# The keys' scales through PSUM in a fused DeltaNet and gated feed-forward kernel

## The chip, the cores and the metric

The kernel runs on one core of one Trainium2 chip. The metric is the device time of one execution in microseconds (us). Three runs of the kernel before took 640.12, 641.81 and 644.32 us; their median is 641.81.

The core's engines work beside each other, each through its own queue in order: PE (matmuls and transposes, results to PSUM), DVE (vector), ACT (activations and copies), POOL (GpSimd), and SP, which here only issues DMAs. They wait for each other through semaphores.

## What is computed

The first part is a DeltaNet layer over 4 batches, 8 heads, 768 steps and heads of 48 numbers; its output, 3072 tokens by 384, goes through a feed-forward layer with the gate h·cos(h) and 2048 hidden features.

```
k_n = k / (np.linalg.norm(k, axis=-1, keepdims=True) + 1e-06)
state = np.zeros((B, H, D, D))
for t in range(S):
    kt, vt, bt = (k_n[:, :, t], v[:, :, t], beta[:, :, t, None])
    y[:, :, t] = np.einsum('bhd,bhde->bhe', q[:, :, t], state)
    v_old = np.einsum('bhde,bhd->bhe', state, kt)
    state = state + bt[:, :, :, None] * np.einsum('bhd,bhe->bhde', kt, vt - v_old)
x = y.transpose(0, 2, 1, 3).reshape(B * S, H * D)
h = x @ w_in
out = (h * np.cos(h)) @ w_out
```

## The kernel before

**Stages.** The 768 steps are cut into 24 units `n` of 32 steps; two units make a pair `m`, and a pair of units is also one block `p` of 256 tokens of the feed-forward layer, so there are 12 blocks. For a unit the kernel loads k, q and v, turns k and q (`turn`, `turn_out`, or from unit 8 on `turn_blocks` on DVE), forms products of keys with keys and queries (`gram`, L652), inverts a triangular 32 by 32 system per head, and solves, updates the state and reads it (`through_state` L907, `right_side` L924, `solve` L979, `solve_out` L991, `update` L1004, `update_out` L1012, `within`). The inversion of the first pair is made by repeated doubling on PE and DVE (L691 to L756), that of the second for half its size, its first columns on DVE, and from then on it runs column by column on POOL: `invert` makes a product (L856, tile `part`) and subtracts it (L863, tile `z`). Its input passes through DRAM (`gram_put`, `gram_get`, tile `gb`), as does its result (`put`, `get`, tile `zt`).

The feed-forward layer of block 0 and of the input side of block 1 is plain (`hidden`, L1076, and `output`, L1274). From then on both of its matrix products are made with fewer multiplications: sums of inputs (`x_sum` L1165), factors on PE (`layer`, L1250), sums of results (`layer_add` L1267), sums of gated blocks (`left_sum` L1348) and of weights (`right_sum` L1361), products on PE (`product`, L1332) and their collection (`collect`, L1371 on ACT, L1384 on DVE). The gate is made by L1113 and L1129 on ACT and L1120 and L1132 on DVE. The weights arrive as 28 tiles (`weights`) and are converted by ACT (L525, L529), DVE (L533) and POOL (`narrow_add`, L537).

**Order.** `Order.LINE` lists all tasks in one order that was written down beforehand; `Order.run` emits them in it, and each engine gets its instructions in that order. `Order.OTHER` says which tasks run on the second of two engines. Nothing is scheduled when the program is built, except the waits: an instruction waits for what it depends on, and for two engines on one PSUM bank the dependency is taken by the bank, not by the columns.

**PSUM.** `p_out` is one bank of 512 columns, declared as [128, 2, 256]. Until the feed-forward output begins, PE runs filler matmuls into it (`keep_warm`, L492), into columns 0 to 255. `output` uses columns 0 to 383, `product` columns 0 to 191 or 256 to 447 by turns. Columns 448 to 511 are not used. A product of the output side has two parts of four matmuls; the next product waits until the previous one is collected.

**Scales of the keys.** For a pair (for the first two pairs: for each unit, "part"), ACT squares the keys (L554), DVE sums them (L559, tile `ksum`), POOL takes the root (L571, tile `knrm`, 8 heads for one or two units: 8 or 16 columns). `scale` on DVE then adds 1e-6 (L582), squares (L584), takes the reciprocal (L585), multiplies by beta (L587, tile `bs`) and spreads that over odd and even quarters (L590, tile `bz`); all five read and write SBUF. There are 14 such groups. `bs` and `bz` go into `gram_keys` (L664, L673) and `solve_out` (L991). `weigh` multiplies v by the norms in place (L607, 128 by 768), from unit 8 on after three small copies (L603, L605) that set the norms of odd heads in place.

Of the kernel before, what the change touches and what calls it, by code (L numbers as in the profile page):

```python
# [10 lines left out]
FP = mybir.dt.float32  # L11
I32 = mybir.dt.int32
U32 = mybir.dt.uint32
ALU = mybir.AluOpType
# [225 lines left out]
def kernel(  # L240
# [32 lines left out]
    nc = tc.nc  # L273

    B, H, S, D = q.shape
# [17 lines left out]
    const = ctx.enter_context(tc.tile_pool(name="const", bufs=1))  # L293
# [3 lines left out]
    work = ctx.enter_context(tc.tile_pool(name="work", bufs=2))  # L297
# [27 lines left out]
    def half(i):  # L325
        return slice(DP * i, DP * i + DP)
# [105 lines left out]
    odd = consts[:, 128 + C : 130 + C]  # L432
# [9 lines left out]
    for b in range(B):  # L442
        nc.gpsimd.dma_start(
            out=bq[C * b : C * b + H].rearrange("p n t -> p (n t)"), in_=beta[b]
# [2 lines left out]

    halves = const.tile([128, 2, H], FP, name="halves")
    nc.vector.memset(halves, 0.5)
    tiny = const.tile([128, 2, H], FP, name="tiny")  # L450
    nc.vector.memset(tiny, 1e-6)
    halfpi = const.tile([128, 1], FP, name="halfpi")
    nc.vector.memset(halfpi, math.pi / 2.0)

# [9 lines left out]
    bt = const.tile([128, NU, H], FP, name="bt")  # L464
# [18 lines left out]

    HM = DM // 2
    p_out = psum.tile([128, 2, 256], FP, name="p_out", tag="o", bufs=1)


    out_begun = []
# [89 lines left out]
    def scale(m, part):  # L578

        n = part.stop - part.start  # L580
        bs, bz, knrm = (t[:, part] for t in scales[m])
        nc.vector.tensor_tensor(out=knrm, in0=knrm, in1=tiny[:, 0:n], op=ALU.add)  # L582
        krec = work.tile([128, 2, H], FP, name="krec")[:, 0:n]
        nc.vector.tensor_tensor(out=krec, in0=knrm, in1=knrm, op=ALU.mult)  # L584
        nc.vector.reciprocal(krec, krec)  # L585
        first = 2 * m + part.start
        nc.vector.tensor_tensor(  # L587
            out=bs, in0=bt[:, first : first + n], in1=krec, op=ALU.mult
        )
        nc.vector.tensor_tensor(  # L590
            out=bz,
            in0=bs[:, :, :, None].to_broadcast([128, n, H, 2]),
            in1=odd[:, None, None, :].to_broadcast([128, n, H, 2]),
            op=ALU.mult,
        )

    def weigh(m):

        vp, knrm = vps[m], scales[m][2]
        if 2 * m >= PLAIN_TURNS:  # L600

            t = work.tile([128, 2, H], FP, name="krec")
            nc.vector.tensor_copy(t[:, :, 0::2], knrm[:, :, 0::2])  # L603
            for i in range(2):
                nc.vector.tensor_copy(t[half(i), :, 1::2], knrm[half(1 - i), :, 1::2])  # L605
            knrm = t
        nc.vector.tensor_tensor(  # L607
            out=vp,
            in0=vp,
            in1=knrm[:, :, :, None].to_broadcast([128, 2, H, D]),  # L610
            op=ALU.mult,
        )

    def turn(n, tag):
# [346 lines left out]
    first, spare = {}, {}  # L961
# [431 lines left out]
    def store(p, i, cols=slice(0, DM)):  # L1393
# [7 lines left out]
        for b in range(B):  # L1401
# [9 lines left out]
            x=2, x_sum=XS, turns=2, g=GATES, o=2, o_out=2,  # L1411
# [59 lines left out]
    def unit(n):  # L1471
# [20 lines left out]
        if n < 4 or not second:  # L1492
            add(("square", m, a), "ACT", 0.2 + 0.37 * width, lambda: norms_square(m, part),
                [("k", 2 * m + x) for x in range(part.start, part.stop)],
                makes=[("g", ("ksq", m, a))])
            add(("sum", m, a), "DVE", 0.2 + 0.4 * width, lambda: norms_sum(m, part),
                [("square", m, a)], makes=[("ksum", ("ksum", m, a))], uses=[("ksq", m, a)])
            add(("norms", m, a), "POOL", 0.4 + 1.28 * width, lambda: norms_root(m, part),
                [("sum", m, a)] + ([("norms", m, 0)] if a else []),
                makes=[] if a else [("scales", ("scales", m))], uses=[("ksum", m, a)])  # L1500
            add(("scale", m, a), "DVE", 1.1, lambda: scale(m, part),
                [("norms", m, a), ("beta",) if n < PLAIN_TURNS else ("beta_home",)])
        scaled = ("scale", m, a if n < 4 else 0)
        if second:
            add(("weigh", m), "DVE", 1.1 if n < PLAIN_TURNS else 1.5, lambda: weigh(m),
                [("v", n - 1), ("v", n), ("scale", m, 0), scaled])
# [419 lines left out]
```

## Time and profile before

| | |
|---|---|
| profiled execution | 641.69 us |
| its span on the core | 639.9 us, so 1.8 us around it |
| granted clock of PE, mean | 0.996 |
| median of three runs | 641.81 us |
| POOL L856 / L863, inversion, 317 each | 142.0 / 141.0 us busy |
| PE L1332 (two groups) / L1250 (four) / L1076 (one of several) | products and factors of the feed-forward layer, the costliest on PE |
| DVE waiting for PE before L1384 | 29.9 us in 34 waits |
| POOL L571, 14 roots | 36.1 us busy, 2.58 us each |
| DMA | 50.36 MB, mean 79 GB/s |

By stages (busy us of each stretch):

| stretch, us | PE | DVE | ACT | POOL |
|---|---|---|---|---|
| 28 to 64 | 32.40 of 36 | 31.96 | 22.59 | 18.97 |
| 64 to 112 | 44.01 of 48 | 29.21 | 25.35 | 38.35 |
| 112 to 172 | 60.00 of 60 | 51.76 | 29.62 | 45.95 |
| 172 to 215 | 40.21 of 43 | 37.67 | 14.78 | 37.73 |
| 215 to 300 | 85.00 of 85 | 68.76 | 40.60 | 72.34 |
| 300 to 400 | 100.00 of 100 | 87.07 | 46.27 | 83.30 |
| 400 to 640 | 236.02 of 240 | 173.19 | 106.79 | 128.16 |

A line of a profile view names the kernel's line (L582 is line 582), the engine, the operation and its tiles as out<-in. In the timeline the first two columns are start and length in us from the start of the span, xN the number of instructions merged into the line (a matmul in fp32 is recorded as two), and what stands in brackets is the idle time of the engine before it and what ended that.

### The profile page before, as it was taken

What the parts mean: (1) busy time and instruction counts of PE and PEld (TensorE: products, weight loads), DVE (VectorE), ACT (ScalarE), POOL (GpSimd) and SP (SyncE); (2) the same over time, 40 slices, a digit from 0 to 9 for tenths busy, and PEclk for the clock granted to TensorE, in tenths of its full rate; (3) what the DMA queues carried; (4) which work ended last, traced back from release to release, by engine and by line L of the source; (5) the groups of instructions that cost most, each with busy time, mean ns of one, the idle gap of its engine ahead of it and who ended that gap; (6) DMA issues with size and microseconds to landing.
All of it is one profiled execution on the core that took longest, in us unless ns stands there. A gap on an engine that the chain in (4) does not pass through costs nothing.

```text
span 639.9 us, 24164 instructions
## 1 busy us (share of the span) xinstructions
PE 618.1 (97%) x10172; PEld 576.0 (90%) x10172; DVE 499.1 (78%) x1026; ACT 298.0 (47%) x528; POOL 435.4 (68%) x779
## 2 busy tenths in 40 slices
PE   6898998999999899999999999999999999999997
PEld 5677878897799899999999999999999999999997
DVE  5799646979788887887988888888888786656682
ACT  3566555555234553634642634743643553545440
POOL 5335977688788888789688888886883883112231
PEclk9999999999999899999999999999999999999999
DMA  7978555843632534424454445243304202000001
GB/s 155 253 157 229 106 128 110 181 87 58 117 46 51 114 50 74 85 55 78 93 79 86 66 73 92 53 64 67 73 3 78 45 2 42 19 3 26 1 24 26
DMA packets 209380, 50.36 MB, mean 79 GB/s; under 512 B 200920, under 2 KB 204280, under 8 KB 209272
## 3 DMA queue, kind: packets, MB, share of 16 engines
q1 hardware_dynamic: 157564, 33.91, 28.2%
q10 hardware_dynamic: 51404, 14.36, 10.8%
q8 instruction: 80, 1.31, 0.8%
q0 software_dynamic: 304, 0.54, 0.4%
q14 instruction: 28, 0.23, 0.1%
HBM read 38.55 MB, written 10.22 MB: 76 GB/s over the span
## 4 chain that ended last, share of the span: by engine, by line
PE 76%; POOL 8%; DMA 5%; DVE 4%; SPq 4%; issue 2%; ACT 0%; POOLq 0%; DVEq 0%
PE p_out L1332 28%; PE p_h L1250 26%; PE p_h L1076 5%; POOL part L856 4%; POOL z L863 4%; PE p_kq L907 3%; PE p_s L1004 3%; PE p_kq L1034 2%; PE p_u L979 2%; PE p_g L652 2%; SPq L396 2%; PE p_h L1332 2%; DMA gb<-g_dr 1%; DMA kp<-in_k_dram 1%; PE p_z L1055 1%
## 5 line engine op out<-in xcount | busy, mean ns | idle before, releaser
L856 POOL TENSOR_TENSOR part<-z,gb 128x126 f32<-128x126 f32 (+24 forms) x317 | 142.0, 448 | 47.0 <-DMA gb<-g_dr 11.7
L863 POOL TENSOR_TENSOR z<-z,part 128x126 f32<-128x126 f32 (+24 forms) x317 | 141.0, 445 | 24.9
L1332 PE MATMUL p_out<-w_out,g_ffn 128*128 128x192 f32 x672 | 123.7, 331 | 0.0
L1332 PEld LDWEIGHTS p_out<-w_out,g_ffn 128*128 128x128 f32 x672 | 108.8, 192 | 1.2 <-DVE g_ffn L1132 0.2
L1129 ACT ACTIVATE turns<-turns,halfpi 128x512 f32<-128x512 f32 x96 | 68.2, 719 | 56.8 <-DVE turns L1120 44.0
L1332 PE MATMUL p_out<-w_sum,g_ffn 128*128 128x192 f32 x496 | 89.8, 329 | 0.2 <-DVE o L1384 0.2
L1250 PE MATMUL p_h<-x_sum,w_in 128*128 128x128 f32 x640 | 83.9, 277 | 1.9 <-POOL x_sum L1165 1.9
L1113 ACT ACTIVATE turns<-g_ffn,quarter_turn 128x512 int32<-128x512 f32 x70 | 50.1, 720 | 69.6 <-DVE g_ffn L1267 23.3
L1250 PEld LDWEIGHTS p_h<-x_sum,w_in 128*128 128x128 f32 x640 | 79.0, 192 | 2.8 <-POOL x_sum L1165 2.1
L1332 PEld LDWEIGHTS p_out<-w_sum,g_ffn 128*128 128x128 f32 x496 | 79.5, 190 | 1.1 <-issue 0.4
L1267 DVE TENSOR_TENSOR g_ffn<-g_ffn,p_h 128x512 f32<-128x512 f32 x80 | 54.1, 680 | 18.5 <-PE p_h L1250 17.4
L1120 DVE SCALAR_TENSOR_TENSOR turns<-g_ffn,turns 128x512 f32<-128x512 f32 x70 | 55.6, 801 | 12.1 <-ACT turns L1113 12.0
L1132 DVE TENSOR_TENSOR g_ffn<-turns,g_ffn 128x512 f32<-128x512 f32 x70 | 53.2, 770 | 4.3 <-ACT turns L1129 4.2
L1047 ACT COPY y<-p_kq 32x384 f32<-32x384 f32 x96 | 45.1, 470 | 20.9 <-PE p_kq L1034 16.9
L1250 PE MATMUL p_h<-x_sum,in_sum 128*128 128x128 f32 x400 | 52.9, 277 | 0.0
L1250 PEld LDWEIGHTS p_h<-x_sum,in_sum 128*128 128x128 f32 x400 | 49.4, 192 | 0.9
L1384 DVE SCALAR_TENSOR_TENSOR o<-p_out,o 128x192 f32<-128x192 f32 x74 | 25.2, 352 | 30.3 <-PE p_out L1332 29.9
L1076 PE MATMUL p_h<-x_ffn,w_in 128*128 128x128 f32 x384 | 46.6, 278 | 1.1 <-DVE part L856 1.1
L1076 PEld LDWEIGHTS p_h<-x_ffn,w_in 128*128 128x128 f32 x384 | 44.2, 192 | 2.3 <-issue 1.2
L571 POOL TENSOR_TENSOR knrm<-ksum,halves 128x16 f32<-128x16 f32 (+1 forms) x14 | 36.1, 2580 | 14.8 <-DVE ksum L559 14.8
L1348 POOL TENSOR_TENSOR g_ffn<-g_ffn,g_ffn 128x512 f32<-128x512 f32 x19 | 27.2, 1434 | 23.2 <-PE p_out L1332 19.4
L1250 PE MATMUL p_h<-x_ffn,w_in 128*128 128x128 f32 x320 | 42.4, 278 | 0.0
(164 smaller groups left out, 1073.4 us busy)
## 6 DMA issues: line engine op xcount, KB each, us to landing
g_ffn<-in_moe_w_out_dram SPq DMA_DIRECT2D x13, 384.0 KB
g_ffn<-in_moe_w_in_dram SPq DMA_DIRECT2D x7, 512.0 KB
vp<-in_v_dram SPq DMA_DIRECT2D x68, 48.0 KB
gb<-g_dr SPq DMA_DIRECT2D x12, 256.0 KB
kp<-in_k_dram SPq DMA_DIRECT2D x120, 24.0 KB
g_ffn<-in_moe_w_in_dram ACTq DMA_DIRECT2D x5, 512.0 KB
zt<-z_dr SPq DMA_DIRECT2D x68, 32.0 KB
out_dram<-o ACTq DMA_DIRECT2D x11, 192.0 KB
```

Of the source, the lines that this page charges most:

```text
L571: nc.gpsimd.tensor_tensor(out=scales[m][2][:, part], in0=sums[m, part.start][:, 0:n], in1=halves[:, 0:n], op=ALU.pow,)
L856: eng.tensor_tensor(out=part, in0=z[:, 0:rows, j, None].to_broadcast(shape), in1=a[:, j, None, j + 1 :].to_broadcast(shape), op=ALU.mult,)
L863: eng.tensor_tensor(out=behind, in0=behind, in1=part, op=ALU.subtract)
L1047: nc.scalar.copy(by_parity(y[quarter(b)]), p_kq[quarter(b ^ 1), :, b % 2])
L1076: nc.tensor.matmul(p_h[:, i], w_in[:, t, (4 * k + i) * 128 : (4 * k + i + 1) * 128], xts[p][:, t, unit * 128 : (unit + 1) * 128], start=(i ...
L1113: nc.scalar.activation(turns[p, f], hidden_of(p, f), AF.Identity, bias=quarter_turn, scale=TURN)
L1120: nc.vector.scalar_tensor_tensor(out=r, in0=hidden_of(p, f), scalar=TURN, in1=t, op0=ALU.mult, op1=ALU.subtract,)
L1129: nc.scalar.activation(r, r, AF.Sin, bias=halfpi, scale=2.0 * math.pi)
L1132: nc.vector.tensor_tensor(out=place(p, f), in0=step_of(rests.pop((p, f)), f), in1=step_of(hidden_of(p, f), f), op=ALU.mult,)
L1250: nc.tensor.matmul(p_h[:, e], in_block(*w)[:, e], x_of(p, b), start=new and e == 0, stop=True, skip_group_check=True,)
L1267: nc.vector.tensor_tensor(out=part_of(p, to), in0=part_of(p, one), in1=part_of(p, two), op=op)
L1332: nc.tensor.matmul(p_o, left(p, part, a)[:, e % 4], right(e, b), start=(e == 0), stop=(e == FT // 2 - 1), skip_group_check=True,)
```

## The change

`krec` moves from a tile of its own in SBUF into the unused columns of `p_out`: 64 columns, of which a group takes 8 or 16 at a place that goes round. `knrm` is no longer changed in place; 1e-6 is added inside the squaring, which now takes two operations (the second adds again and multiplies), and inside `weigh`. `bz` is made from `krec` and beta directly, by two operations with `odd` as a scalar for each partition, one for each of the two columns. `scale` has six operations on DVE for five, each with at most one input from SBUF; `weigh` has the same number, its last a scalar_tensor_tensor of two SBUF inputs. The constant tile `tiny` and its memset go. The order of tasks is the same.

```diff
-    tiny = const.tile([128, 2, H], FP, name="tiny")
-    nc.vector.memset(tiny, 1e-6)
...
     p_out = psum.tile([128, 2, 256], FP, name="p_out", tag="o", bufs=1)
+    spare_out = p_out[:, 1, HM:]
...
         bs, bz, knrm = (t[:, part] for t in scales[m])
-        nc.vector.tensor_tensor(out=knrm, in0=knrm, in1=tiny[:, 0:n], op=ALU.add)
-        krec = work.tile([128, 2, H], FP, name="krec")[:, 0:n]
-        nc.vector.tensor_tensor(out=krec, in0=knrm, in1=knrm, op=ALU.mult)
+
+        at = (2 * m + part.start) % 4 * 2 * H
+        krec = spare_out[:, at : at + n * H].rearrange("p (u h) -> p u h", h=H)
+        nc.vector.tensor_scalar(krec, knrm, 1e-6, None, op0=ALU.add)
+        nc.vector.scalar_tensor_tensor(
+            out=krec, in0=knrm, scalar=1e-6, in1=krec, op0=ALU.add, op1=ALU.mult
+        )
         nc.vector.reciprocal(krec, krec)
         first = 2 * m + part.start
-        nc.vector.tensor_tensor(
-            out=bs, in0=bt[:, first : first + n], in1=krec, op=ALU.mult
-        )
-        nc.vector.tensor_tensor(
-            out=bz,
-            in0=bs[:, :, :, None].to_broadcast([128, n, H, 2]),
-            in1=odd[:, None, None, :].to_broadcast([128, n, H, 2]),
-            op=ALU.mult,
-        )
+        beta_here = bt[:, first : first + n]
+        nc.vector.tensor_tensor(out=bs, in0=beta_here, in1=krec, op=ALU.mult)
+        for x in range(2):
+            nc.vector.scalar_tensor_tensor(
+                out=bz[:, :, :, x], in0=krec, scalar=odd[:, x : x + 1], in1=beta_here,
+                op0=ALU.mult, op1=ALU.mult,
+            )
...
-        nc.vector.tensor_tensor(
+        nc.vector.scalar_tensor_tensor(
             out=vp,
-            in0=vp,
-            in1=knrm[:, :, :, None].to_broadcast([128, 2, H, D]),
-            op=ALU.mult,
+            in0=knrm[:, :, :, None].to_broadcast([128, 2, H, D]),
+            scalar=1e-6,
+            in1=vp,
+            op0=ALU.add,
+            op1=ALU.mult,
         )
```

## The prediction, made before the result

> **What bounds the kernel now.** I read the page first: its busy times and its chain.
>
> ```profile
> PE 618.1 (97%) x10172; PEld 576.0 (90%) x10172; DVE 499.1 (78%) x1026; ACT 298.0 (47%) x528; POOL 435.4 (68%) x779
> PE 76%; POOL 8%; DMA 5%; DVE 4%; SPq 4%; issue 2%; ACT 0%; POOLq 0%; DVEq 0%
> ```
>
> PE is busy nearly throughout and is three quarters of the chain, so a microsecond counts only if it makes PE start its next matmul earlier or later. From 112 us until its last matmul the PE timeline shows three idle gaps (0.78 at 172, 1.94 at 214, 0.20 at 440), 2.9 us together: there, whatever stalls PE is added one for one.
>
> Next I asked for the lines of the small operations (duration ns, min/median/max).
>
> ```profile
> L584 DVE TENSOR_TENSOR krec<-knrm x14: 166/175/1222, 11.4 to 450.0; 128x16 f32<-128x16 f32 x10, 128x8 f32<-128x8 f32 x4
> L585 DVE RECIPROCAL krec<-krec x14: 202/252/253, 11.6 to 450.2; 128x16 f32<-128x16 f32 x10, 128x8 f32<-128x8 f32 x4
> L673 DVE TENSOR_TENSOR g<-p_g,bs x22: 380/416/426, 34.0 to 485.7; 128x256 f32<-128x256 f32 x22
> ```
>
> With two inputs from SBUF (L584) an operation is sometimes seven times its median; with one (L585), or one of two from PSUM (L673), never. The timeline shows what it is then waiting for.
>
> ```profile
> 52.47 5.04 POOL L537 TENSOR_TENSOR w_in<-w_in,g_ffn 128x512 uint32<-128x512 uint32 x4 [0.70 <-DVE w_in L533]
> 53.12 0.67 DVE L582 TENSOR_TENSOR knrm<-knrm,tiny 128x16 f32<-128x16 f32 x1
> 53.82 1.22 DVE L584 TENSOR_TENSOR krec<-knrm 128x16 f32<-128x16 f32 x1
> 55.36 0.93 DVE L587 TENSOR_TENSOR bs<-bt,krec 128x16 f32<-128x16 f32 x1
> 56.32 1.23 DVE L590 TENSOR_TENSOR bz<-bs,consts 128x32 f32<-128x32 f32 x1
> 57.48 0.16 DVE L856 TENSOR_TENSOR part<-z,gb 128x15 f32<-128x15 f32 x1
> ```
>
> Four POOL additions run back to back, and one DVE operation gets through behind each. The scale group takes 4.4 us here; an undisturbed one (124.59) takes 1.1.
>
> **The change, part by part.** *Length of a group.* Five operations become six: the undisturbed starts are 0.20, 0.21, 0.29 and 0.21 us apart and the last takes 0.19; the new sixth adds one more 0.2, so 1.3 us for 16 columns a partition, 1.24 for 8. Nothing in this trace writes PSUM from DVE; L1384, which reads 192 columns of PSUM in 0.36 us, lies on the slope of SBUF operations (0.17 for 16 columns, 0.28 for 128), so I take no surcharge. Bounds: 0 and, if every write cost as much again as the operation, +0.8. Thirteen groups pay 0.2 us more; DVE's own idle time (22% of the span) covers that, and without that cover it would be 2.6 us. The scaling of v (L607) becomes a scalar_tensor_tensor of the same shape: L1120, such a form on SBUF, takes 0.68 for 512 columns, as does the tensor_tensor L1132; nothing. The removed memset is 0.07 us before PE has work.
>
> *Relief at 53.12.* In DVE 3.1 us. Of this PE can recover the two gaps it has there, 1.08 us before 59.72 and 1.21 before 63.84: at most 2.3. But what follows in DVE's queue is L856 and L863, the inversion's products, with both inputs in SBUF. The new group would end at 54.45; the additions end at about 53.73, 54.99, 56.25 and 57.51, so the first three products get through at 55.0, 56.3 and 57.55, and the fourth, which started at 58.10 before, at 57.55. Gain: 0.55 us, between 0 and 2.3. I take 0.55, since these products are the form that was held.
>
> *New waits.* The intermediate now lies in the bank of p_out, and in the built program the group's first operation waits for the last p_out matmul ahead of it, and the next p_out matmul waits for the group's last operation. I set each of the fourteen groups beside the p_out matmuls. Where DVE arrives first:
>
> ```profile
> 364.35 0.38 DVE L582 TENSOR_TENSOR knrm<-knrm,tiny 128x16 f32<-128x16 f32 x1
> 365.67 0.73 DVE L924 SCALAR_TENSOR_TENSOR rhs<-p_kq,consts,vp 128x192 f32<-128x192 f32 x2
> 365.43 1.47 PE L1332 MATMUL p_out<-w_out,g_ffn 128*128 128x192 f32 x8
> 368.61 0.68 PE L979 MATMUL p_u<-rhs,zt 64*64 64x48 f32 x32
> 372.10 0.89 PE L1004 MATMUL p_s<-u,kp 64*64 64x96 f32 x32
> ```
>
> At 364.35 the group must wait until the product ends at 366.90; it ends at 368.3. Queued behind it are L924's four, 1.4 us: the right side is ready at 369.7, and PE's solve, at 368.61, is 1.1 us late. Then u (L991) ends near 374.0 where 372.1 wanted it: up to 2.1 in all. I take 1.6. At 330.74 the wait is until 332.53; the group ends at 333.9, and behind it L1165, L1267 and the collect L1384 end at 335.05, while PE's next product, which waits for that collect, began at 334.14: 1.0 (0 to 1.85, the whole lag). At 287.97 the wait is 1.75 us, but PE's next product began at 292.22 and the collect would be done at 291.5: nothing. At 88.01 the wait is 0.6: the state update L1012 moves from 89.47 to 90.0, and PE's L652 already waits for it: 0.5 (0 to 0.6).
>
> Where PE arrives first:
>
> ```profile
> 34.93 1.13 PE L492 MATMUL p_out<-o 128*128 128x256 f32 x4
> 35.80 0.15 DVE L582 TENSOR_TENSOR knrm<-knrm,tiny 128x8 f32<-128x8 f32 x1
> 124.59 0.16 DVE L582 TENSOR_TENSOR knrm<-knrm,tiny 128x16 f32<-128x16 f32 x1
> 124.82 2.75 PE L1274 MATMUL p_out<-w_out,g_ffn 128*128 128x384 f32 x8
> ```
>
> The first row is two filler matmuls; the second, at 35.46, must wait for the group of 35.80, until 37.04 plus the 0.15 us by which PE followed DVE's L991 at 47.33. PE's queue is solid from 28.7 to 47 and DVE waits for PE at 39.61, so this is 1.7 us (0 to 1.7). At 124.82 the product must wait until 126.0: 1.1 (0 to 1.3); PE has no gap between 109 and 172. The other groups have room: at 53.12 PE's filler comes at 55.50, at 189.66 the product at 192.61, at 213.64 at 216.56, at 423.30 at 425.51, at 449.78 at 452.14. The first three lie ahead of 28.68, where PE stood idle 1.26 us for q from DRAM; that wait covers the 1.9 us by which the filler at 10.58 and the transposes behind it are held, except for what passes 1.26 (0 to 0.6; I take 0, since their product is wanted only at 15.90).
>
> Sum: 1.7 − 0.55 + 0.5 + 1.1 + 1.0 + 1.6 = +5.35 us. The profiled execution took 641.69, a span of 639.9 and 1.8 around it, 0.1 from the median of 641.81: I forecast **647.0**.
>
> One thing the sum leaves out is the clock: over 212.0 to 215.4 PE was busy 1.46 us of 3.40, and over 215.4 to 219.0 the granted clock was 0.53. The stalls above are up to 1.7 us in one place. Each such stretch costs about 1.7 us (half of 3.4). The Trainium skill (TensorE: Matmul & The Clock Gate, Why this matters for your kernels) asks for no idle gaps over about 3 us; by that none of the stalls here would cost clock, and the sum would stay. The trace goes against it: the drop came behind a gap of 1.94 us, though none came behind the 2.67 us before 14.83.
>
> **Rivals.** *Relief wins* (not slower): if the products let through at 55 to 57.5 are not held, PE gets 2.3 us at 64, and if DVE drifts by half a microsecond against PE, the wait at 88.01 falls away and those at 124.82 and 330.74 halve. Then 1.7 − 2.3 + 0 + 0.5 + 0.5 + 0 = +0.4 with the right side at 364 hidden too: 642. For it: PE's own gaps at 59.72 and 63.84. Against: L856 and L863 have the form of the held operations. It decides once the inversion's first product starts before 56.
>
> *Clock drops* (slower by over 1%): two of the new stalls pull the clock down for 3.4 us each, +3.4: 650.4. For: the row at 215.4. Against: the gap at 14.83, and that the longest new stall is 1.7. It decides from PE being busy under 45% of one 3.4 us stretch.
>
> *The change relieves nothing*: if an operation with one PSUM operand is held like the others, the group at 53.12 stays at 4.4 us and the waits remain: +5.9, 647.6. Against it stand the three rows on L584, L585 and L673.
>
> **Chances.** About 1% (6.4 us: below 635.4, above 648.2) is what a measurement of this kernel can tell from no change. The sum has 0.55: most of its bounds lie under 648.2, so 0.40 within and 0.15 above. Relief wins 0.20: 0.16 within, and 0.04 faster, which would need every held operation to have been on PE's path. Clock drops 0.17, all slower. No relief 0.08: 0.05 within, 0.03 slower. Together faster 0.04, within 0.61, slower 0.35. The range reaches from the relief case with a microsecond below it, 641, to the clock case with half a microsecond above, 651.
>
> **What would show it.** In the profile of after: the group at about 55 us takes 1.3 us and none of its operations over 0.3; the first inversion products behind it take over 1 us each; PE shows gaps of about 1.7 us before a filler near 35.5, 1.1 before the product near 126, 1.0 near 336, and about 1.1 before the solve near 372, all named after DVE's scale lines or what stands behind them. If those gaps are missing the sum is wrong; if the gaps are there but the span isn't longer, PE had slack that the timeline doesn't show.

## The result, and the profile after

The kernel after takes 644.69 us (median of 15 runs, 642.89 to 649.42) beside 640.93 us for the kernel before (15 runs on the same chip, 639.08 to 644.32). The ratio is 1.0066 with a 95% interval of 1.0047 to 1.0085: 4.2 us slower, 3.0 to 5.4. Forecast were 647.0 us and +5.35.

The profiled execution of after is the slowest of its fifteen, 649.42 us with a span of 647.6; places in its trace are compared below, not its total. First the page: busy times, and the chain that ended last by engine.

```profile
PE 620.7 (96%) x10172; PEld 577.4 (89%) x10172; DVE 497.7 (77%) x1039; ACT 298.1 (46%) x528; POOL 435.9 (67%) x779
PE 77%; DVE 11%; DMA 4%; POOL 3%; SPq 2%; issue 2%; ACT 0%; ACTq 0%; DVEq 0%; POOLq 0%
```

DVE has 13 instructions more and is busy 1.4 us less: its scale lines take 15.9 us together where they took 19.4. In the chain DVE went from 4% to 11%: PE now follows DVE at more places.

Three of the five scale lines on DVE (duration in ns, min/median/max, then first and last start):

```profile
L593 DVE SCALAR_TENSOR_TENSOR bz<-p_out,consts,bt x28: 216/224/228, 12.2 to 458.7; 128x16 f32<-128x16 f32 x20, 128x8 f32<-128x8 f32 x8
L584 DVE TENSOR_SCALAR p_out<-knrm x14: 148/170/179, 11.5 to 457.7; 128x16 f32<-128x16 f32 x10, 128x8 f32<-128x8 f32 x4
L585 DVE SCALAR_TENSOR_TENSOR p_out<-knrm,p_out x14: 170/178/180, 11.7 to 458.0; 128x16 f32<-128x16 f32 x10, 128x8 f32<-128x8 f32 x4
```

None is ever held: the longest L585 takes 180 ns, where its forerunner L584 took up to 1222. But see what follows the group beside POOL's four additions, in the timeline:

```profile
54.28 5.05 POOL L536 TENSOR_TENSOR w_in<-w_in,g_ffn 128x512 uint32<-128x512 uint32 x4 [0.70 <-DVE w_in L532]
54.93 0.15 DVE L584 TENSOR_SCALAR p_out<-knrm 128x16 f32<-128x16 f32 x1
55.72 0.37 DVE L593 SCALAR_TENSOR_TENSOR bz<-p_out,consts,bt 128x16 f32<-128x16 f32 x2
56.01 0.86 DVE L859 TENSOR_TENSOR part<-z,gb 128x15 f32<-128x15 f32 x1
56.90 1.21 DVE L866 TENSOR_TENSOR z<-z,part 128x15 f32<-128x15 f32 x1
58.15 1.23 DVE L859 TENSOR_TENSOR part<-z,gb 128x28 f32<-128x28 f32 x1
59.41 0.19 DVE L866 TENSOR_TENSOR z<-z,part 128x28 f32<-128x28 f32 x1
```

The group is over in 1.2 us, and the next three operations, products and differences of the inversion with two inputs from SBUF, are held in its place until the additions end at 59.33. The fourth is free.

Now PE's timeline, the rows with idle time ahead of them (in brackets: how long, and what ended it):

```profile
37.18 0.70 PE L491 MATMUL p_out<-o 128*128 128x256 f32 x2 [1.41 <-DVE bz L593]
61.03 2.92 PE L1079 MATMUL p_h<-x_ffn,w_in 128*128 128x128 f32 x24 [0.58 <-DVE part L859]
65.15 1.13 PE L982 MATMUL p_u<-rhs,w_sum 64*64 64x48 f32 x32 [1.21 <-DVE w_sum L759]
92.09 0.86 PE L655 MATMUL p_g<-kq_t 48*32 48x64 f32 x64 [0.50 <-DVE st L1015]
99.54 0.63 PE L622 MATMUL p_t<-consts,qp 128*128 128x128 f32 x4 [1.26 <-DMA qp<-in_q_dram]
129.26 2.82 PE L1277 MATMUL p_out<-w_out,g_ffn 128*128 128x384 f32 x8 [0.89 <-DVE bz L593]
178.15 2.06 PE L982 MATMUL p_u<-rhs,zt 64*64 64x48 f32 x32 [1.60 <-DMA zt<-z_dr]
222.92 1.57 PE L1335 MATMUL p_out<-w_out,g_ffn 128*128 128x192 f32 x8 [1.46 <-DVE bz L593]
340.76 1.57 PE L1335 MATMUL p_out<-w_sum,g_ffn 128*128 128x192 f32 x8 [0.76 <-DVE o L1387]
375.82 0.95 PE L982 MATMUL p_u<-rhs,zt 64*64 64x48 f32 x32 [0.51 <-PE p_h L1253]
380.14 0.89 PE L1007 MATMUL p_s<-u,kp 64*64 64x96 f32 x32 [0.23 <-DVE u L994]
```

Three gaps end with bz, the last operation of a scale group, and the one at 340.76 with the collect behind a group. Two end with a DMA; the sum of the prediction has no term for them. Two rows of DVE's timeline show the other side, where a group comes first and waits for a product in p_out:

```profile
338.46 0.18 DVE L584 TENSOR_SCALAR p_out<-knrm 128x16 f32<-128x16 f32 x1 [1.93 <-PE p_out L1335]
373.56 0.18 DVE L584 TENSOR_SCALAR p_out<-knrm 128x16 f32<-128x16 f32 x1 [2.75 <-PE p_out L1335]
```

I set the start of each matmul of after beside the same one of before. PE's lag at times of before: 0.1 us ahead of 35.46; 1.8 behind that filler; 1.3 at 59.72; 1.6 at 90.48; 3.3 at 96.25; 4.5 at 124.82; 5.3 at 172.82; 6.9 at 176 and 5.3 again at 214; 5.6 at 257 and 5.8 at 330; 6.6 at 334.14; 8.0 at 372.10; 7.7 at the end.

### The profile page after: what moved, and what is told of

It is laid out like the page before. It is cut to its first block, busy times and chain, and to the rows that moved or that the text cites. A ratio compares the mean times of both kernels' runs of the same rounds, so it can differ in the third digit from the quotient of the medians.

```text
span 647.6 us, 24188 instructions
## 1 busy us (share of the span) xinstructions
PE 620.7 (96%) x10172; PEld 577.4 (89%) x10172; DVE 497.7 (77%) x1039; ACT 298.1 (46%) x528; POOL 435.9 (67%) x779
## 4 chain that ended last, share of the span: by engine, by line
PE 77%; DVE 11%; DMA 4%; POOL 3%; SPq 2%; issue 2%; ACT 0%; ACTq 0%; DVEq 0%; POOLq 0%
PE p_out L1335 29%; PE p_h L1253 26%; PE p_h L1079 4%; PE p_kq L910 3%; PE p_s L1007 3%; PE p_kq L1037 2%; PE p_u L982 2%; PE p_g L655 2%; DMA kp<-in_k_dram 2%; PE p_h L1335 2%; POOL z L866 1%; POOL part L859 1%; PE p_z L1058 1%; PE p_h L739 1%; SPq L882 1%
## 5 line engine op out<-in xcount | busy, mean ns | idle before, releaser
L866 POOL TENSOR_TENSOR z<-z,part 128x126 f32<-128x126 f32 (+24 forms) x317 | 142.6, 450 | 24.8
L1335 PE MATMUL p_out<-w_out,g_ffn 128*128 128x192 f32 x672 | 122.4, 328 | 1.5 <-DVE bz L593 1.5
L1351 POOL TENSOR_TENSOR g_ffn<-g_ffn,g_ffn 128x512 f32<-128x512 f32 x19 | 27.2, 1436 | 22.8 <-PE p_out L1335 19.0
```

Of the source, the lines that this page charges most:

```text
L866: eng.tensor_tensor(out=behind, in0=behind, in1=part, op=ALU.subtract)
L1335: nc.tensor.matmul(p_o, left(p, part, a)[:, e % 4], right(e, b), start=(e == 0), stop=(e == FT // 2 - 1), skip_group_check=True,)
```

## Experiments

Waits theory: the added time is the waits of p_out matmuls and scale groups for each other, less a small relief. Rivals: the rewritten arithmetic, or a relief that is whole and hidden by the waits. Each kernel was timed beside before on the same chip, 10 to 12 runs beside 17 to 35.

| kernel | median, us | before, us | ratio, 95% interval |
|---|---|---|---|
| sbuf_all | 639.99 | 640.27 | 0.9984 (0.9964 to 1.0004) |
| psum_g4 | 641.03 | 640.27 | 1.0006 (0.9985 to 1.0027) |
| psum_pe_first | 641.80 | 640.27 | 1.0018 (0.9994 to 1.0043) |
| psum_dve_first | 642.88 | 640.27 | 1.0033 (1.0009 to 1.0057) |
| psum_early | 641.53 | 640.84 | 1.0007 (0.9985 to 1.0030) |
| psum_room | 640.33 | 640.84 | 0.9984 (0.9965 to 1.0003) |
| g4_reorder | 642.40 | 640.84 | 1.0018 (1.0000 to 1.0036) |
| sbuf_reorder | 643.98 | 640.84 | 1.0050 (1.0029 to 1.0071) |
| after_q | 648.10 | 641.50 | 1.0081 (1.0053 to 1.0110) |
| g4_reorder_q | 642.40 | 641.50 | 1.0012 (0.9984 to 1.0040) |
| sbuf_q | 643.78 | 641.50 | 1.0033 (1.0009 to 1.0056) |
| psum_eight | 642.25 | 641.57 | 1.0015 (0.9986 to 1.0043) |

An interval is 1.2 to 1.8 us to each side, so single terms of the sum can be seen only when they add up; where a term is smaller, the trace has to say where PE started later.

**krec in SBUF everywhere (sbuf_all).**

```diff
-        krec = spare_out[:, at : at + n * H].rearrange("p (u h) -> p u h", h=H)
+        krec = work.tile([128, 2, H], FP, name="krec")[:, 0:n]
```

> The changed kernel with its intermediate krec back in SBUF in all fourteen groups; the six operations stay, the waits through p_out's bank and the relief go. Waits theory (the added time is the waits of p_out matmuls and scale groups for each other, less a small relief): within 1 us of the kernel before, about +0.3. Rival 'the rewritten arithmetic costs it' (one operation more in each group, the scaling of v as scalar_tensor_tensor): stays at about +4. In the profile the group near 53 us takes 4 to 5 us again.

Measured −1.0 us against before (0.9984 times 641), interval −2.3 to +0.3. The six operations are all there and cost nothing; that rival falls. The timeline of its DVE beside POOL's additions (52.92 to 57.96):

```profile
53.58 0.68 DVE L584 TENSOR_SCALAR krec<-knrm 128x16 f32<-128x16 f32 x1
54.29 1.23 DVE L585 SCALAR_TENSOR_TENSOR krec<-knrm,krec 128x16 f32<-128x16 f32 x1
55.55 0.25 DVE L588 RECIPROCAL krec<-krec 128x16 f32<-128x16 f32 x1
58.07 0.16 DVE L859 TENSOR_TENSOR part<-z,gb 128x15 f32<-128x15 f32 x1
```

The group takes 4.6 us again and the inversion behind it is free. Even the first operation, which has one input, is held: 0.68 us where the same into PSUM took 0.15. In the group at 215.06 it takes 1.06 us, until an operation of POOL (L1351, 214.81 to 216.08) has ended. The Trainium skill (SBUF — State Buffer, Who interferes with whom) has both: an operation with at most one SBUF input doesn't contend with GpSimd, except tensor_scalar and copies in their two-port modes, which can. These rows agree with it; that L584 ran in such a mode no row shows.

**PSUM in one part of the groups.** Five kernels, of this form; the list names the groups that keep PSUM, the others have krec in SBUF:

```diff
+        if (m, part.start) in [(2, 0)]:
             krec = spare_out[:, at : at + n * H].rearrange("p (u h) -> p u h", h=H)
+        else:
+            krec = work.tile([128, 2, H], FP, name="krec")[:, 0:n]
```

The list is [(2, 0)] in psum_g4, [(1, 1), (4, 0)] in psum_pe_first, [(3, 0), (7, 0), (8, 0), (9, 0)] in psum_dve_first, [(0, 0), (0, 1), (1, 0)] in psum_early and [(5, 0), (6, 0), (10, 0), (11, 0)] in psum_room.

> PSUM for krec in one group alone, the one that lay beside POOL's four additions at 53.12 us before; the other thirteen in SBUF. Waits theory with the contention moved on: the group takes 1.3 us, the inversion's first products behind it over 0.8 us each, and the time is 0.55 us under that of krec in SBUF everywhere. Rival 'the relief is whole and was only hidden by the waits': 2.3 us under it. Rival arithmetic: no difference.

Measured +0.4 against before and 1.0 over sbuf_all by the medians: no gain, where even 0.55 was expected. In its trace PE's gap ahead of the hidden product is 0.57 us (1.22 in sbuf_all), and that ahead of the solve is 1.21 in both. PE does get half a microsecond at that place; the 2.3 of the rival it doesn't get, and nothing of it is seen at the end: its lead over sbuf_all goes at 172 us (0.5, where PE waits for the inverse from DRAM) and at 214 (0.5, and 3.4 us at half clock behind it).

> PSUM for krec in the groups at 35.80 and 124.59 us alone, where PE comes to its p_out matmul first and must wait for the group. Waits theory: +1.7 and +1.1, so 2.8 us over krec in SBUF everywhere; PE shows a gap near 36.5 us and one near 126.5, each ended by bz. Rival arithmetic: no difference to SBUF everywhere.

Measured +1.2 against before and 1.8 over sbuf_all by the medians (2.8 expected). Both gaps are in PE's timeline, the second in this execution longer than the 1.1 forecast:

```profile
36.82 0.70 PE L491 MATMUL p_out<-o 128*128 128x256 f32 x2 [1.48 <-DVE bz L596]
131.99 2.82 PE L1280 MATMUL p_out<-w_out,g_ffn 128*128 128x384 f32 x8 [1.62 <-DVE bz L596]
```

> PSUM for krec in the groups at 88.01, 287.97, 330.74 and 364.35 us alone, where DVE comes first and must wait for a p_out product. Waits theory: 0.5 + 0 + 1.0 + 1.6 = 3.1 us over krec in SBUF everywhere, from what is queued behind the group on DVE; the place at 364 gives half of it. A rival within the theory, that DVE catches up since it is idle a fifth of the time: under 1 us. Rival arithmetic: no difference.

Measured +2.1 against before, 2.9 over sbuf_all by the medians (3.1 expected). PE's timeline shows the forecast places:

```profile
91.14 0.86 PE L658 MATMUL p_g<-kq_t 48*32 48x64 f32 x64 [0.50 <-DVE st L1018]
98.67 0.63 PE L625 MATMUL p_t<-consts,qp 128*128 128x128 f32 x4 [1.63 <-DMA qp<-in_q_dram]
336.19 1.57 PE L1338 MATMUL p_out<-w_sum,g_ffn 128*128 128x192 f32 x8 [0.76 <-DVE o L1390]
371.25 0.95 PE L985 MATMUL p_u<-rhs,zt 64*64 64x48 f32 x32 [0.52 <-PE p_h L1256]
375.43 0.89 PE L1010 MATMUL p_s<-u,kp 64*64 64x96 f32 x32 [0.16 <-DVE u L997]
```

Against sbuf_all its PE loses 0.2 us at 91, 0.8 at 336 and 1.3 from 371 to 376, 2.4 us at the forecast places. Another 1.8 came at the transposes at 98.67, where q from DRAM is late, and 0.8 at the solve at 175, which waits for the inverse from DRAM; this execution is one of the kernel's slower ones, 4.6 us above the one of sbuf_all. So the forecast places are shown, but the 2.9 us of the medians need not be these places alone. Catching up, the rival within the theory, hardly happens: of the 4.8 us of lag at 376 PE wins back 0.2.

> PSUM for krec in the first three groups alone, all ahead of 28.68 us. The prediction took their waits as covered by PE's wait for q from DRAM: 0 (up to +0.6) against krec in SBUF everywhere. Rival: the filler held near 10.6 us passes the cover, up to +1.9.

Measured +0.4 against before, some 1.5 over sbuf_all (1.0007 less 0.9984); the interval of that difference, about 1.9 to each side, holds both 0 and 1.9. In its trace the filler does move, from 10.58 to 12.75 us, and the transposes behind it by 2.7 to 3.1; at 28.68 PE is 1.5 us ahead of before. In this execution the wait was covered; what it costs on average stays open.

> PSUM for krec in the groups at 189.66, 213.64, 423.30 and 449.78 us alone, which the prediction took to have room: 0 against krec in SBUF everywhere. The changed kernel's trace shows PE idle 1.46 us before its product at 222.92, ended by bz: by that reading the place at 213.64 costs 1.0 us and the others nothing, so +1.0. Either way the gap that PE had near 214, and the clock's drop behind it, may go or stay; each stretch of half clock counts 1.7 us of its own.

Measured 0.0 against sbuf_all (0.9984 both). At 213.64 the product waits 0.29 us for bz here; PE's gap at 215, ended by ACT in this trace, is 1.44. The 1.46 us that after shows at 222.92 stood beside another gap that went, so the place costs nothing in sum.

**What lies behind the relief (g4_reorder, sbuf_reorder).** Three moves in the written order, in both kernels: the right side (169) behind the scale group (250), the first inversion columns (224) behind the doubling's first addition (167), the second addition (165) to its factors (164) and the next columns (225) behind it.

```diff
-... 249 250 224 162
-2119 2115 163 2133 272 166 167 273 30 2103 31 225 160 253 2136 161 2111 164 792 2125 169 2123 300
-254 2140 255 165 2144 170 226 ...
+... 249 250 169 162
+2119 2115 163 2133 272 166 167 224 273 30 2103 31 160 253 2136 161 2111 164 165 225 792 2125 2123
+300 254 2140 255 2144 170 226 ...
```

> PSUM for krec in the group beside POOL's four additions alone, and three steps of DVE's queue moved: the right side of the solve (operations that read one input from PSUM) goes straight behind this group, the first inversion columns behind the doubling's first addition, the next columns behind its second. Nothing else moves on any engine. Contention theory: the operations that now lie beside the additions aren't held, the inversion's products come after them, and PE loses its gaps of 0.58 and 1.21 us before the hidden product and the solve: 1.8 us under the same kernel without the moves, some 2.3 under the kernel before. Rival 'the relief is worth nothing to PE whatever follows': no difference to the kernel without the moves.

> The same three moves with krec in SBUF everywhere. Contention theory: the group itself is held for 4 us or more, so the first gap stays and only the second, before the solve, goes: 1.2 us under krec in SBUF everywhere, 1.1 behind the moves together with PSUM in that one group. Rival 'the moves alone do it': equal to those with PSUM.

Both misses. g4_reorder came out at +1.2 against before, 0.8 over psum_g4; sbuf_reorder at +3.2. The timeline of g4_reorder, first DVE, while POOL's additions run from 52.98 to 58.02, then PE:

```profile
54.71 0.73 DVE L930 SCALAR_TENSOR_TENSOR rhs<-p_kq,consts,vp 128x192 f32<-128x192 f32 x2
55.36 0.73 DVE L930 SCALAR_TENSOR_TENSOR rhs<-p_kq,consts,rhs 128x192 f32<-128x192 f32 x2
56.13 0.42 DVE L762 TENSOR_TENSOR w_sum<-w_sum,p_h 128x256 f32<-128x256 f32 x1
56.84 1.21 DVE L869 TENSOR_TENSOR z<-z,part 128x15 f32<-128x15 f32 x1
```

```profile
62.52 1.14 PE L985 MATMUL p_u<-rhs,w_sum 64*64 64x48 f32 x32 [0.49 <-DVE tt L798]
97.30 1.09 PE L625 MATMUL p_t<-consts,qp 128*128 128x128 f32 x4 [2.12 <-DMA qp<-in_q_dram]
```

The contention theory holds: operations with one input from PSUM run beside the additions unheld, the gap ahead of the hidden product is gone, and PE's solve starts 1.9 us earlier than in sbuf_all (62.52 against 64.44). But at the transposes it stands idle for 2.12 us and is later than sbuf_all by 0.4. The reason can be followed in part: the columns that DVE inverts end at 61.71 us (60.51 in psum_g4), the transfer of z to DRAM goes out 4.9 to 5.2 us after that in every trace, and behind it in SP's queue come the inverse and then q (L396). The last of q's four is issued at 95.39, in psum_g4 at 92.62. I took this for a second path, from the inversion through DRAM, that meets PE there. But in sbuf_all the columns end later still, at 62.10, and q is in time: the first of its four is issued at 89.73, as in g4_reorder (89.64), and the four take SP 4.02 us, where they take 6.06 in g4_reorder. So against sbuf_all it is the issuing of q that is slower, and why is not shown. What PE gained ahead of it is taken back.

In sbuf_reorder the solve's gap is 1.70 us and ended by tt, not by the addition that was moved: the solve's p_u needs the PSUM bank that p_g held until tt was read out. Its profiled execution is its fastest, so where the rest of its 3.2 us lies is not shown; the clock, below, is part of it.

**q ahead of the inverse (after_q, g4_reorder_q, sbuf_q).** The task ('q', 7) moves ahead of ('get', 3), in after, in g4_reorder and in sbuf_all:

```diff
-796 2155 807 197 354 2156 198 199 200 800 832 229 2160 ...
-204 809 324 810 ...
+796 2155 807 197 354 2156 198 199 200 800 832 324 229 2160 ...
+202 204 809 810 ...
```

> The changed kernel, with one step of SP's queue moved: the four transfers of q that the transposes near 96 us read go ahead of the eight that fetch the inverse for turn 3; nothing else moves on any engine. Theory of a second path (the end of the first inversion, its way through DRAM, then q behind it in SP's queue, meets PE at those transposes): q lands 4 to 5 us earlier, PE's gap of 1.26 us before them goes, 1.6 us under the changed kernel, if the inverse isn't late in its place (PE wants it near 100 us). Rival 'the DMA engines are the limit there and only the order changes': no difference, or the solve of turn 3 waits for the inverse.

> PSUM for krec in the one group, the three moves in DVE's queue, and q ahead of the inverse in SP's queue. Theory of a second path: the 1.9 us that the moves gained until 64 us are no longer taken back at the transposes near 96 us, where this kernel without the last move stood idle 2.12 us for q: some 2 us under it and 1.5 under the kernel before. Rival as for the changed kernel with q moved: no difference; a third place that takes the gain back would be the inverse near 172 us, where the kernel before stood idle 0.78 us.

> krec in SBUF everywhere and q ahead of the inverse in SP's queue. Here q was in time, so the theory of a second path gives no difference to krec in SBUF everywhere; a gain of a microsecond or more would say that q's place is worth something by itself, a loss that the inverse becomes late.

All three are misses: after_q is at +5.2 against before (1.0 over after, within the interval), g4_reorder_q at +0.8 with an interval from −1.0 to +2.6, and sbuf_q is 3.1 over sbuf_all (1.0033 less 0.9984). PE has no gap for q in any of them; the timeline of after_q in order of time, ACT's queue, ACT, then PE:

```profile
91.08 3.07 ACTq L396 DMA_DIRECT2D vp<-in_v_dram  x4
94.19 1.92 ACT L1050 COPY y<-p_kq 32x384 f32<-32x384 f32 x4 [4.86 <-DMA vp<-in_v_dram]
96.16 1.15 PE L910 MATMUL p_kq<-st,kq_t 48*64 48x48 f32 x64 [0.65 <-ACT y L1050]
97.74 0.60 PE L622 MATMUL p_t<-consts,qp 128*128 128x128 f32 x4
103.00 1.84 PE L940 MATMUL p_w<-rhs,w_sum 32*32 32x48 f32 x64 [1.74 <-ACT kq_t L632]
```

Issuing four transfers of v takes ACT 3.07 us here (1.84 in after, 1.85 in sbuf_all, 3.50 in g4_reorder_q), ACT copies y later, and the copy of kq_t behind the weights' conversions makes PE wait 1.74 us at 103. The rival stands, that another order of transfers only moves the wait; that the DMA engines as a whole are the limit between 84 and 104 us fits these rows, but wasn't tried by itself.

**PSUM in eight groups (psum_eight).** The list is [(0, 0), (0, 1), (1, 0), (2, 0), (5, 0), (6, 0), (10, 0), (11, 0)].

> The changed kernel with krec in SBUF in the six groups alone at which a wait was priced above nothing or found to cost (those at 35.80, 124.59, 88.01, 287.97, 330.74 and 364.35 us before); the other eight, the one beside POOL's additions among them, keep PSUM. Waits theory: all that the change adds sits in these six, so 4 us under the changed kernel and within 1 us of the kernel before. Rival 'a cost spread over all fourteen groups' (writing PSUM, one operation more): 14 - 6 = 8 of 14 groups still pay, some 2.4 us over the kernel before.

Measured +1.0 against before, 3.3 under after, interval −0.9 to +2.8: as the waits theory has it, but the rival's 2.4 lies inside. The profiled span is 638.6 us, and from 256 us on its PE starts within 0.3 us of sbuf_all's. No kernel tried beats before by more than its interval.

The five kernels with PSUM in one part of the groups hold all fourteen between them. By the ratios they are 1.4, 2.2, 3.1, 1.5 and 0.0 us over sbuf_all (in the order of their list), 8.2 in sum, where after is 5.3 over it. The intervals allow that difference, so what single parts cost is known only to within a microsecond or two.

## Why the prediction was right

*Length of a group: nothing.* Right: sbuf_all has six operations and takes no longer, and writing PSUM costs 0.15 to 0.18 us an operation, the reciprocal 0.27 for 0.25, which is no surcharge to speak of.

*Relief 0.55.* The mechanism was right: three of the inversion's operations are let through one by one, ending at 56.87, 58.11 and 59.38, the fourth free. PE's lag falls by 0.5 us at 59.72 and its gap ahead of the solve stays 1.21. As a term of the total it was too large: psum_g4 isn't faster than sbuf_all, and in the traces of psum_g4 and g4_reorder PE loses its lead again at later waits, for the inverse, for POOL and for q. The rival "relief wins" asked for products that aren't held; the first started at 56.01 and was held, so this rival falls.

*Filler at 35.46: 1.7.* Right: the lag grows by 1.7 there. *Product at 124.82: 1.1.* Right, 1.1 in the lag. Together the runs give 1.8 us for 2.8 forecast; the two kernels compared have intervals of 1.6 and 1.3 us to each side.

*88.01: 0.5.* The lag grows by 0.3 at 90.48. *330.74: 1.0.* Nearly right, 0.8. *287.97: 0.* Right. *364.35: 1.6.* Right in sum, 1.4 in three steps (0.58, 0.54 and 0.30 at 368.6, 369.5 and 372.1). The gap before the solve is 0.51 and not 1.1: the group took 1.2 us from the product's end and not 1.4, and the solve starts 0.2 us before the last of the right side's four operations ends (376.04). Together 2.9 us by the medians and 2.4 in the trace of psum_dve_first, 3.1 forecast.

*Groups with room.* Right as a sum (psum_room), though at 213.64 PE did wait for bz: I had compared the group with the product in before's time only, and in after the two stand differently to each other. *The first three groups, covered.* Right in the traces, where PE is within 0.2 us or ahead at 28.68; in time not settled.

*What was left out.* The sum has no term for the transfers. In the profiled execution 1.4 us came at the transposes at 96.25, where q was late, and 0.8 at the solve at 172.82, where the inverse was; gaps of 1.6 to 2.1 us for q stand in psum_pe_first, psum_dve_first and g4_reorder too. The sum of the terms as seen in the lag, 1.7 − 0.5 + 0.3 + 1.1 + 0.8 + 1.4 = 4.8, is above the 4.2 by the ratio, though the transfers come on top of it in that execution; what takes the rest back in an average run is not shown. So the direction and the places were foreseen, and that the number came this near is in part luck. Of the 2.3 us between 647.0 and 644.69, 0.8 is the start (641.69 for a kernel whose median is 640.93 over the later runs) and the other 1.6 the sum, 5.35 where the medians differ by 3.8.

*Clock drops.* Not in the time. Two stretches at half clock appear in the profiled execution of after: one from 11.5 us, at the start, where psum_g4 and psum_room have one too (from 16.2 and 16.8 us) without PSUM in the first groups, and one from 178.8, behind the wait for the inverse. None stands behind a stall that was priced, though in psum_pe_first one does, behind the filler at 36.82. Over its fifteen runs the mean granted clock is 0.996, as before's is in the later runs (0.994 to 0.996): after loses no more to it than before. *The change relieves nothing* fell with the group's 1.2 us.

## What to carry to other kernels

Spare columns of a PSUM bank aren't free storage: a group of small operations there can wait for the bank's other user and make it wait, and each such meeting has to be priced by who comes first and what is queued behind. An operation that is no longer held gives its place to the next of the same form in the queue. A gain on the critical engine counts only if the next place where that engine waits for something else, here transfers, doesn't take it back.

## What the hardware showed that I had not expected

The clock can fall after shorter pauses than I had allowed for. The windows of after, then of psum_pe_first, g4_reorder and sbuf_reorder (length, busy time of PE, PEld, DVE, ACT and POOL, granted clock, DMA share and GB/s):

```profile
175.50:178.90 3.40, 1.72 (x23) 1.46 (x23) 3.40 (x8) 1.16 (x2) 1.27 (x1) 0.98 0.78 120
178.90:182.30 3.40, 3.40 (x34) 3.31 (x32) 1.85 (x4) 0.00 (x0) 2.82 (x8) 0.51 0.49 95
```

```profile
34.40:37.80 3.40, 1.92 (x27) 1.12 (x24) 3.26 (x14) 0.44 (x1) 0.00 (x0) 1.00 0.68 158
37.80:41.30 3.50, 3.50 (x34) 2.52 (x32) 0.83 (x3) 0.37 (x1) 0.00 (x0) 0.51 0.77 164
```

```profile
93.40:96.80 3.40, 1.78 (x68) 1.45 (x64) 2.66 (x7) 2.04 (x6) 2.85 (x8) 0.98 0.44 59
96.80:100.20 3.40, 2.90 (x14) 2.93 (x15) 0.88 (x2) 3.00 (x7) 2.93 (x7) 0.52 0.50 79
```

```profile
60.40:63.80 3.40, 1.70 (x37) 1.54 (x36) 3.07 (x10) 0.98 (x2) 1.26 (x5) 0.99 0.82 222
63.80:67.20 3.40, 3.40 (x25) 3.31 (x21) 2.43 (x6) 0.00 (x0) 2.69 (x11) 0.50 0.18 28
```

Each of these times PE was busy 1.70 to 1.92 us of 3.4, with a longest pause of 1.48 to 2.12 us, and then ran at half clock for about 3.4. In sbuf_all PE was busy 2.01 of 3.40 us from 211.4 on, and the clock stayed at 1.00; after's pause of 1.46 at 222.92 brought no drop either (1.95 of 3.40). My condition, under 45% busy, was too strict: 56% was enough here. But a low share doesn't always bring a drop: in psum_pe_first PE was busy 1.68 us of 3.40 from 99.3 on and 1.78 from 130.0 on, with pauses of 1.72 and 1.62 us, and the clock stayed at 1.00.

```profile
130.00:133.40 3.40, 1.78 (x9) 1.09 (x8) 3.08 (x11) 2.17 (x4) 2.65 (x9) 1.00 0.92 289
133.40:136.80 3.40, 3.40 (x46) 2.54 (x45) 1.40 (x3) 1.92 (x4) 2.78 (x8) 1.00 0.65 96
```

So neither the pause nor the busy time alone decides, and what does is not shown. The Trainium skill (TensorE: Matmul & The Clock Gate, Why this matters for your kernels) speaks of idle gaps over about 3 us; the four drops above differ from it, and decide.

Over all runs the mean granted clock is 0.992 in sbuf_reorder and 0.993 in after_q, g4_reorder_q and sbuf_q, beside 0.994 to 0.996 in before and 0.997 in sbuf_all: by (1 − clock) times 640 us, sbuf_reorder loses 5.0 us where before loses 2.9. So up to two of its 3.2 us are clock, by this reckoning. By the same reckoning sbuf_q loses 2.8 us more than sbuf_all and after_q 2.0 more than after, which is most of sbuf_q's 3.1 and more than after_q's 1.0. The reckoning is high rather than low: between runs of one kernel, all thirteen sets together, a clock lower by 0.001 went with 0.33 us, not 0.64. In after_q the half clock lasted from 103.5 to 113.8 us.
